# Output projection in the body as pairs of 64-row products, with a change of PSUM banks halfway

## The chip, the core and the metric

The kernel runs on one core of a Trainium2 chip. The metric is the device time of one execution in microseconds; the median of several runs is given, and one execution was profiled. The core's engines are TensorE (PE in the profile; its weight loads are PEld), VectorE (DVE), ScalarE (ACT), GpSimd (POOL) and SyncE (SP), which issues most of the DMAs.

## What is computed

For each of 8 batches, with S = 3200 rows, D = 256 columns and 64 inner columns:

```python
# stage 1, attention with squared ReLU, gated by u
scores = (1 / S) * z @ z.T                 # 3200 x 3200
x = u * (np.maximum(scores, 0.0) ** 2 @ v) # 3200 x 256
# stage 2, a mixing over the tokens, then the output projection
wq, wk = x @ w_q, x @ w_k                  # 3200 x 64 each
mixed = (1 / np.sqrt(64)) * (wq @ wk.T) @ x
out = np.maximum(mixed, 0.0) @ w_out       # 3200 x 256
```

Inputs and output are fp32; the kernel multiplies in fp16 and adds in fp32 in PSUM.

## The kernel before

**Tiling.** The 3200 rows of a batch are 25 tiles of 128, and seven groups: six of 512 rows (W) and one of 128 (LASTG). A step of the main product takes 64 of a tile's 128 rows on the upper half of TensorE's rows and the other 64 on the lower half: two products with 64 rows each, written `top(0)` and `top(1)`, that run side by side and add into two PSUM banks, acc{half}0 and acc{half}1. Nearly every product of the body has this 64-row form.

**The parts, by line.** `scores` (L224) makes a pair of score tiles, sc, in a PSUM tile of two banks. `first_stage` (L243 on ScalarE, L247 on VectorE) takes ReLU into g; `second_stage` (L260 on ScalarE, L262 on GpSimd) squares into at. Part of the tiles are turned by DMA transposes into tt (L282), as the score matrix is symmetric. `second_product` (L303) is the main product into acc. `gate` adds the two acc banks (L319 on ScalarE, then L320 on VectorE) and multiplies by u on GpSimd (L335). Then follow the transposed x (L349), the projections qk (L366, L379), the keys (L384), the heads hd (L393), and, a batch later, `mix` (L429), whose ReLU `mix_out` writes into rt on ScalarE (L446), and `proj` (L456), the output projection: for a group of 512 rows, four tiles of 128 rows times two chunks of 128 columns, 8 products of 128 rows each, against the weights wo. `proj_out` scales the two banks in one ScalarE pass (L484) into fo, and SP stores it (L485).

**PSUM.** The four acc banks are the main product's. The other four are two tiles of two banks each, tag ps, which sc, qk, hd, mx and fo take in turn.

**What sets the order.** The schedule is manual: every engine takes its instructions in the order in which the program writes them. A planner in Python writes them. It keeps a clock for TensorE, VectorE, ScalarE and GpSimd (`clock`), adds planned durations with `give`, and holds planned times for SP and the transfers (`sp_at`, `dma_at`, `moves`). Its main loop (L862 to L895) looks at TensorE's planned time and chooses what it does next: an "extra" (keys, heads, mix, proj), a score pair, or one step of the main product. Score pairs and extras need a free PSUM tile; `slots` holds the times at which the two tiles are planned to be free again, `open_slot` takes the first and `close_slot` puts a time back. Score pairs may run ahead of the main product by a lead of 140 steps. For a projection, `use_proj` plans 1.08 us of TensorE and 1.0 us of ScalarE for a large group. The plan only orders instructions; at run time semaphores hold each one until its data are there.

The body has 47 such projections, 40 of 512 rows and 7 of 128. Batch 7's own, and two groups of batch 6 that are kept back, are projected in the tail, behind the main loop, by `projected` and `proj`; the tail is the same before and after.

Of the kernel before, what the change touches and what calls it, by code (L numbers as in the profile page):

```python
# [10 lines left out]
FP32 = mybir.dt.float32  # L11
RELU = mybir.ActivationFunctionType.Relu
AOP = mybir.AluOpType
# [3 lines left out]
def kernel(  # L17
# [10 lines left out]
    nc = tc.nc  # L28

    B, S, D = u.shape  # L30
    dqk = z.shape[2]
    dh = moe_w_q.shape[1]
    P = 128
# [48 lines left out]
    def top(r):  # L82
        return slice(r * dqk, (r + 1) * dqk)
# [5 lines left out]
    def rows(t, b):  # L89
        return t[b].rearrange("(p n) d -> p n d", n=NT)  # L90
# [10 lines left out]
    def load_first_z():  # L101
        for i, (n0, nn) in enumerate(ZCH):
            z32[n0] = px.tile([P, nn, dqk], FP32, tag="x_sb", name="z32")
            queue = nc.scalar if i == 1 else nc.sync
            queue.dma_start(out=z32[n0][:], in_=rows(z, 0)[:, n0 : n0 + nn, :])
# [342 lines left out]
    def proj(b, gi, banks):  # L448
        rt = rts.pop((b, gi))
        nj = widths[gi] // P  # L450
        for r in halves(gi):
            n = min(2, nj - 2 * r)
            flat = rt[:, r, :, :].rearrange("p d s -> p (d s)")
            for dc in range(ND):
                for j in range(n):
                    nc.tensor.matmul(  # L456
                        out=banks[r][:, ds(j * D, D)],
                        lhsT=flat[:, ds((dc * n + j) * P, P)],
                        rhs=wo[:, dc, :],
                        start=(dc == 0 and j == 0),  # L460
                        stop=(dc == ND - 1 and j == n - 1),
                    )

    def proj_out(b, gi, banks, ways, stores=None):
        n0 = starts[gi] // P
        if stores is None:
            fo = pg.tile([P, 2, W], FP32, tag="g", name="fo")
        else:
            fo = pg.tile([P, 2, W], FP32, tag="fo", name="fo", bufs=2)
        flat_out = fo[:].rearrange("p a w -> p (a w)")  # L470
        at = 0
        for on_dve, queue, n in ways:
            sl = slice(at * D, (at + n) * D)
            if isinstance(banks, list):
                part = banks[at // 2][:, 0 : n * D]
            else:
                part = banks[:].rearrange("p a w -> p (a w)")[:, sl]
            if on_dve:
                nc.vector.tensor_scalar(
                    out=flat_out[:, sl], in0=part, scalar1=FINAL_SCALE, scalar2=None,  # L480
                    op0=AOP.mult,
                )
            else:
                nc.scalar.mul(out=flat_out[:, sl], in_=part, mul=FINAL_SCALE)  # L484
            store = lambda queue=queue, at=at, n=n, sl=sl: queue.dma_start(  # L485
                out=rows(out, b)[:, n0 + at : n0 + at + n, :],
                in_=flat_out[:, sl].rearrange("p (n d) -> p n d", d=D),
            )
            if stores is None:
                store()  # L490
            else:
                stores.append(store)
            at += n
# [29 lines left out]
    def give(engine, ready, weight):  # L523
        clock[engine] = max(clock[engine], ready) + weight
        return clock[engine] + HOP

    slots = [0.0, 0.0]
    free_at, row_at, blocks = {}, {}, {}
    pending, later, extras, keyed, kept = [], [], [], [], []
    out_of, turned_at, z_at = {}, {}, {}  # L530
    produced, stored = [0], []
    last = B - 1

    moves = []
    sp_at, dma_at = [0.0], [0.0]
    LANDS = 4.0
    RING = 2.0
# [34 lines left out]
            send(min(ripe, key=lambda x: x[1]))  # L572

    def open_slot():
        clock[PE] = max(clock[PE], slots.pop(0))

    def close_slot(t):
        slots.append(t)

    def cold():  # L580
        return 2.0 if clock[PE] < 11.0 else 1.0

    def use_pair():
        open_slot()
        p = produced[0]
        produced[0] += 1
        sc = scores(p)
        clock[PE] += 0.22 * cold()
        ready = clock[PE] + FROM_PE
        on_act = max(clock[ACT], ready) + BIAS < max(clock[DVE], ready)  # L590
        done = give(ACT, ready, 1.03) if on_act else give(DVE, ready, 1.2)
        g = first_stage(p, sc, on_act)
        close_slot(done)
        pending.append((done, p, g))

    def squares():
# [20 lines left out]
                row_at[b, gj, starts[gi] // P + n] = t + 0.5  # L617

    def use_keys(b, gi):
        open_slot()  # L620
        ps = ps_tile("qk")
        projections(b, gi, ps)
        clock[PE] += 0.44 if gi < LASTG else 0.24
        ready = clock[PE] + FROM_PE
        projections_out(b, gi, ps)
        done = give(ACT, ready, 0.56)
        n = widths[gi] / P
        move(
            done + SLACK, done + 10.0, 1.28, 0.21 * n, lambda: turn_keys(b, gi),
            lambda t: at_time(t, lambda: keys_landed(b, gi)), lambda: len(ks) < NK,  # L630
        )
        close_slot(done)

    FIRST_HEADS = range(3)

# [4 lines left out]
                add_extra(clock[PE] + 0.5, "heads", lambda gis=gis: use_heads(b, gis))  # L640

    def use_heads(b, gis):
        open_slot()
        ps = ps_tile("hd")
        heads(b, gis, ps)
        clock[PE] += 0.2 + 0.0547 * sum(widths[gi] // P for gi in gis)
        heads_out(b, ps)
        done = give(DVE, clock[PE] + FROM_PE, 0.7)
        close_slot(done)
        if gis is FIRST_HEADS:  # L650
            return
        done = give(DVE, done, 0.35)
        move(done + SLACK, done + 2.0, 0.55, 0.1, lambda: cross_heads(b, 0))
        move(
            done + SLACK, done + 2.0, 0.55, 0.1, lambda: cross_heads(b, 1),
            lambda t: at_time(t, lambda: crossed(b)),
        )
# [14 lines left out]
                    add_extra(t + 4.0 + 18.0 * i, "mix", lambda gi=gi: use_mix(b, gi))  # L672

    def use_mix(b, gi):
        open_slot()
        ps = ps_tile("mx")
        mix(b, gi, [ps[:, 0, :], ps[:, 1, :]])
        clock[PE] += 0.22
        mix_out(b, gi, ps)
        done = give(ACT, clock[PE] + FROM_PE, 1.03 if gi < LASTG else 0.3)  # L680
        close_slot(done)
        add_extra(done + 0.5, "proj", lambda: use_proj(b, gi))

    def use_proj(b, gi):
        open_slot()
        ps = ps_tile("fo")
        proj(b, gi, [ps[:, 0, :], ps[:, 1, :]])
        clock[PE] += 1.08 if gi < LASTG else 0.42
        stores = []
        proj_out(b, gi, ps, [(False, nc.sync, widths[gi] // P)], stores)  # L690
        done = give(ACT, clock[PE] + FROM_PE, 1.0 if gi < LASTG else 0.3)
        close_slot(done)
        stored.append(1e9)

        def landed(t, i=len(stored) - 1):
            stored[i] = t

        move(done + SLACK, done + 6.0, 0.55, 1.6, stores[0], landed)
# [128 lines left out]
        return all(x in used for x in tiles[2 * p : 2 * p + 2])  # L827

    make_identity(nc, ident)
    load_first_z()  # L830
    load_first_v(0, 2)
    cast_first(0)
# [29 lines left out]
    while groups or work or current["left"]:  # L862
        flush()
        squares()
        now = clock[PE]
        room = slots[0] <= now
        extra = next(
            (
                x
                for x in extras  # L870
                if x[0] <= now
                and (x[1] != "proj" or len(stored) < 2 or stored[-2] <= now)
                and (x[1] != "mix" or sum(y[1] == "proj" for y in extras) < 2)
            ),
            None,
        )
        p = produced[0]
        able = p < NPAIR and z_at[p_chunk(p)] <= now and (p < NAT or all_used(p - NAT) and turned_at.get(p - NAT, 0.0) <= now and not out_of.get(p - NAT))
        wanted = able and p * total < (done_acc + lead) * NPAIR
        room = room and calm(1.1)  # L880
        if room and extra and (not wanted or turn_about or extra[1] == "proj"):
            turn_about = False
            extras.remove(extra)
            extra[2]()
        elif room and wanted:
            turn_about = True
            use_pair()
        elif acc_step():
            done_acc += 1
        elif room and able:  # L890
            use_pair()
        else:
            marks = [slots[0], sp_at[0] - 0.4] + [x[0] for x in pending + later + extras + moves]
            marks += list(free_at.values()) + [t for t in row_at.values() if t > now][:50]
            clock[PE] = min([t for t in marks if t > now] + [now + 0.5])  # L895

    while extras or later or moves:
        x = next((x for x in extras if x[1] == "proj"), None)  # L900
        if not x:
            ripe = [x for x in moves if not x[6] or x[6]()]
            x = min(later + extras + ripe, key=lambda x: x[0])
        clock[PE] = max(clock[PE], x[0])
        if x in later:
            later.remove(x)
            x[1]()
        elif x in moves:
            send(x)
        else:  # L910
            extras.remove(x)
            x[2]()
# [74 lines left out]
```

## Time and profile before

| | us |
|---|---|
| median of 3 runs | 791.21 (791.0 to 795.83) |
| profiled execution, its time | 790.96 |
| its span, first to last instruction | 789.2 |
| TensorE busy (PE) | 763.2 (97%) |
| weight loads (PEld) | 645.7 (82%) |
| VectorE | 479.4 (61%) |
| ScalarE | 551.8 (70%) |
| GpSimd | 612.9 (78%) |

The granted TensorE clock is 0.994 in the mean. A busy TensorE is not TensorE at its peak, as products overlap and their ends are modelled. In a row of the groups or of the timeline stand the engine, the line, the operation, what it writes and reads, shapes, counts and times; "[0.21 <-issue]" is idle time ahead of an instruction and what ended it, "issue" being a wait for nothing that the profile shows. In the table of waits a row gives the sum in us, the times, and the longest.

### The profile page before, as it was taken

The numbers are of one execution on the slowest core, as the hardware profiler recorded it, in microseconds if no ns is written. First come the engines' busy times: TensorE is split into PE (matmuls) and PEld (weight loads), VectorE is DVE, ScalarE is ACT, GpSimd is POOL, SyncE is SP. The second block draws the span as 40 slices with busy tenths as digits, with TensorE's granted clock in tenths as the row PEclk, the third lists the DMA queues.
The fourth block names the chain that finished last, engine by engine and source line by source line (L and its number), as shares of the span: only waits on it lengthen the run. The fifth ranks groups of instructions, "written<-read, shape, count | busy, mean of one in ns | idle before, by whom it ended". The sixth has DMA issues, their size and how long they took to land.

```text
span 789.2 us, 28159 instructions
## 1 busy us (share of the span) xinstructions
PE 763.2 (97%) x12373; PEld 645.7 (82%) x12373; DVE 479.4 (61%) x479; ACT 551.8 (70%) x659; POOL 612.9 (78%) x418
## 2 busy tenths in 40 slices
PE   6989999999999999999999999999999999999976
PEld 5879898887888888888788887988788888888864
DVE  5755577664685656754587635666468654675634
ACT  5766478766776677786687678866778767777624
POOL 7887799886998769877798876888789775787830
PEclk9999999999999999999999999999999999999998
DMA  7999999999999979999999999999999998899425
GB/s 192 146 172 165 177 160 179 156 225 194 204 184 189 220 164 194 152 189 216 210 162 170 187 214 199 177 151 208 193 207 165 178 225 160 183 163 194 122 56 220
DMA packets 310636, 142.57 MB, mean 181 GB/s; under 512 B 287985, under 2 KB 291953, under 8 KB 310513
## 3 DMA queue, kind: packets, MB, share of 16 engines
q1 hardware_dynamic: 303600, 124.60, 83.4%
q0 software_dynamic: 6768, 15.98, 14.8%
q8 instruction: 96, 1.57, 0.9%
q14 instruction: 28, 0.22, 0.1%
q10 hardware_dynamic: 144, 0.20, 0.1%
HBM read 59.64 MB, written 26.21 MB: 109 GB/s over the span
## 4 chain that ended last, share of the span: by engine, by line
PE 91%; DVE 3%; DMA 2%; issue 1%; ACT 1%; POOL 1%; SPq 0%; DVEq 0%; POOLq 0%; ACTq 0%
PE acc L303 66%; PE sc L224 12%; PE fo L456 6%; PE qk L366 3%; DVE g L247 2%; PE hd L393 1%; PE mx L429 1%; DVE both L320 1%; DMA v_sb<-in_v_dram 1%; DMA hx<-ha 1%; ACT both L319 1%; POOL x_sb L335 1%; DVE ha L410 0%; DMA z<-in_z_dram 0%; SPq L349 0%
## 5 line engine op out<-in xcount | busy, mean ns | idle before, releaser
L262 POOL TENSOR_TENSOR at<-g 128x1024 f16<-128x1024 f32 (+2 forms) x245 | 451.5, 1858 | 82.5 <-DVE g L247 66.5
L303 PE MATMUL acc<-v_sb,at 64*128 64x256 f16 x7312 | 499.1, 270 | 5.0 <-DVE both L320 2.5
L247 DVE TENSOR_SCALAR g<-sc 128x1024 f32<-128x1024 f32 (+2 forms) x309 | 363.9, 1197 | 153.0 <-PE sc L224 137.6
L303 PEld LDWEIGHTS <-at 64*128 64x128 f16 x7312 | 393.0, 94 | 66.8 <-issue 12.7
L260 ACT ACTIVATE at<-g 128x1024 f16<-128x1024 f32 x223 | 229.4, 1036 | 30.7 <-DVE g L247 27.2
L243 ACT ACTIVATE g<-sc 128x1024 f32<-128x1024 f32 (+1 forms) x159 | 159.2, 1003 | 60.5 <-PE sc L224 59.8
L335 POOL TENSOR_TENSOR x_sb<-both,u_sb 128x512 f16<-128x512 f32 (+1 forms) x112 | 134.4, 1207 | 64.4 <-DVE both L320 63.8
L224 PE MATMUL sc<-zT 64*128 64x512 f16 x920 | 180.2, 378 | 3.5 <-DVE g L247 3.1
L303 PE MATMUL acc<-v_sb,tt 64*128 64x256 f16 x2304 | 158.7, 269 | 0.0
L320 DVE TENSOR_TENSOR both<-acc,both 128x512 f32<-128x512 f32 (+1 forms) x104 | 69.1, 670 | 128.9 <-ACT both L319 128.4
L303 PEld LDWEIGHTS <-tt 64*128 64x128 f16 x2304 | 123.3, 94 | 11.6 <-issue 0.4
L319 ACT COPY both<-acc 128x512 f32<-128x512 f32 (+1 forms) x104 | 58.4, 566 | 65.5 <-PE acc L303 63.5
L224 PEld LDWEIGHTS <-zT 64*128 64x128 f16 x920 | 56.8, 94 | 17.6 <-issue 12.4
L484 ACT ACTIVATE fo<-fo 128x1024 f32<-128x1024 f32 (+2 forms) x50 | 44.9, 908 | 23.5 <-PE fo L456 22.1
L446 ACT ACTIVATE rt<-mx 128x1024 f16<-128x1024 f32 (+1 forms) x49 | 45.1, 931 | 22.1 <-PE mx L429 21.8
L456 PE MATMUL fo<-wo,rt 128*128 128x256 f16 x400 | 53.1, 276 | 1.2 <-ACT rt L444 0.6
L456 PEld LDWEIGHTS <-rt 128*128 128x128 f16 x400 | 35.4, 98 | 15.6 <-issue 9.6
L379 ACT CAST qk<-qk 128x512 f16<-128x512 f32 (+1 forms) x54 | 29.4, 544 | 21.6 <-PE qk L366 21.6
L366 PE MATMUL qk<-xT_sb,wqk 64*128 64x256 f16 (+1 forms) x404 | 32.2, 265 | 0.1
L366 PEld LDWEIGHTS <-wqk 64*128 64x128 f16 x416 | 22.8, 94 | 2.5 <-issue 0.5
L303 PE MATMUL acc<-v_sb,ttl 64*128 64x256 f16 x384 | 24.6, 269 | 0.0
L303 PEld LDWEIGHTS <-ttl 64*128 64x128 f16 x384 | 19.7, 94 | 3.5 <-issue 0.8
(42 smaller groups left out, 163.9 us busy)
## 6 DMA issues: line engine op xcount, KB each, us to landing
u_sb<-in_u_dram SPq DMA_DIRECT2D x48, 512.0 KB, 5.1
out_dram<-fo SPq DMA_DIRECT2D x45, 512.0 KB, 4.7
v_sb<-in_v_dram POOLq DMA_DIRECT2D x35, 320.0 KB, 6.0
zn<-in_z_dram POOLq DMA_DIRECT2D x7, 400.0 KB, 5.7
tt<-at SPq DMA_TRANSPOSE x144, 4.4
out_dram<-fo SPq DMA_DIRECT2D x6, 256.0 KB, 2.1
u_sb<-in_u_dram SPq DMA_DIRECT2D x8, 128.0 KB, 3.9
hx<-ha SPq DMA_DIRECT2D x16, 64.0 KB, 4.7
```

What stands on the lines that cost most here:

```text
L224: nc.tensor.matmul(out=sc[:, h, 0:gw], lhsT=zT[b][top(h), ts(ti, P)], rhs=zT[b][top(h), ds(gs, gw)], start=True, stop=True,)
L243: nc.scalar.activation(out=g[:, hs, 0:w], in_=sc[:, hs, 0:w], func=RELU, scale=GSCALE)
L247: nc.vector.tensor_scalar(out=g[:, hs, 0:w], in0=sc[:, hs, 0:w], scalar1=0.0, scalar2=GSCALE, op0=AOP.max, op1=AOP.mult,)
L260: nc.scalar.square(out=out, in_=g[:, hs, 0:w])
L262: nc.gpsimd.tensor_mul(out=out, in0=g[:, hs, 0:w], in1=g[:, hs, 0:w])
L303: nc.tensor.matmul(out=accs[half, r][:, ds((j % 2) * D, D)], lhsT=weights(b, gi, ti, j)[top(r), :], rhs=vs[b][top(r), ti, :], start=(first ...
L319: nc.scalar.copy(out=both[:, 0 : n * D], in_=accs[half, 0][:, 0 : n * D])
L320: nc.vector.tensor_add(out=both[:, 0 : n * D], in0=accs[half, 1][:, 0 : n * D], in1=both[:, 0 : n * D])
L335: nc.gpsimd.tensor_mul(out=xs[b, gi][:, 0:n, :, r, :].rearrange("p n c d -> p (n c) d"), in0=both[:, 0 : n * D].rearrange("p (m d) -> p m ...
L366: nc.tensor.matmul(out=ps[:, r, 0 : n * P], lhsT=wqk[top(r), c, :, :].rearrange("p t h -> p (t h)"), rhs=xTs[b, gi][top(r), 0:n, c, :], st ...
L446: nc.scalar.activation(out=out, in_=ps[:, 0:nr, 0 : ND * n * P], func=RELU)
L456: nc.tensor.matmul(out=banks[r][:, ds(j * D, D)], lhsT=flat[:, ds((dc * n + j) * P, P)], rhs=wo[:, dc, :], start=(dc == 0 and j == 0), sto ...
```

## The change

The body's projections take the 64-row form. `proj_stage` runs in two stages for a large group. In stage 0 the upper 64 rows of the first half of the row tiles add into bank 0, and, side by side with them, the lower 64 rows of the second half into bank 1. In stage 1 the banks change places: the upper rows work for the second half, into bank 1, the lower rows for the first half, into bank 0. [...] The planner puts other work between the stages; stage 1 is a new kind of entry, `changes`, which the main loop takes first once its planned time has come. The PSUM tile stays taken until stage 1 has been scaled; an open tile has the time 1e9 in `slots`.

A group of 128 rows has one stage: each 64-row half has a bank of its own, and `small_proj_out` adds the two, ScalarE scaling one and VectorE adding the other. Two tiny tiles, signs, are cleared by GpSimd at the start. The planned times are 0.44 us of TensorE a stage and 0.22 us for a small group.

```diff
+    signs = [consts.tile([1, 2], FP32, tag=f"sign{i}", name=f"sign{i}") for i in range(2)]
+    SEES = mybir.DependencyInfo(mybir.DependencyClass.Sync, mybir.DependencyReason.DATA)
+
+    def proj_stage(b, gi, ps, stage, seen=None):
+        rt = rts[b, gi]
+        nj = widths[gi] // P
+        n = min(2, nj)
+        product = None
+        for dc in range(ND):
+            for j in range(n):
+                for r in range(2):
+                    bank = r ^ stage
+                    half = bank if nj > n else 0
+                    flat = rt[:, half, :, :].rearrange("p d s -> p (d s)")
+                    product = nc.tensor.matmul(
+                        out=ps[:, bank, ds(j * D, D)],
+                        lhsT=flat[top(r), ds((dc * n + j) * P, P)],
+                        rhs=wo[top(r), dc, :],
+                        start=(stage == 0 and dc == 0 and j == 0),
+                        stop=(dc == ND - 1 and j == n - 1 and (stage == 1 or nj == n)),
+                    )
+                    if seen is not None:
+                        tc.add_manual_dep(
+                            product.ins, seen.ins.name, SEES, reason="the change of halves"
+                        )
+                        seen = None
+        return product
+
+    def sign_off(product, on_act):
+        sign = signs[0 if on_act else 1]
+        copy = nc.scalar.copy if on_act else nc.vector.tensor_copy
+        seen = copy(out=sign[:, 1:2], in_=sign[:, 0:1])
+        tc.add_manual_dep(seen.ins, product.ins.name, SEES, reason="last before the change")
+        return seen
+
+    def small_proj_out(b, gi, ps, stores):
+        n0 = starts[gi] // P
+        fo = pg.tile([P, 2, W], FP32, tag="fo", name="fo", bufs=2)
+        nc.scalar.mul(out=fo[:, 0, 0:D], in_=ps[:, 0, 0:D], mul=FINAL_SCALE)
+        nc.vector.scalar_tensor_tensor(
+            out=fo[:, 0, 0:D], in0=ps[:, 1, 0:D], scalar=FINAL_SCALE, in1=fo[:, 0, 0:D],
+            op0=AOP.mult, op1=AOP.add,
+        )
...
-    slots = [0.0, 0.0]
+    slots = [[0.0], [0.0]]
...
+    moves, changes = [], []
+    SEEN = 0.1
...
     def open_slot():
-        clock[PE] = max(clock[PE], slots.pop(0))
-
-    def close_slot(t):
-        slots.append(t)
+        slot = slots.pop(0)
+        assert slot[0] < 1e9
+        clock[PE] = max(clock[PE], slot[0])
+        slot[0] = 1e9
+        slots.append(slot)
+        return slot
+
+    def close_slot(slot, t):
+        slot[0] = t
...
     def use_proj(b, gi):
-        open_slot()
+        slot = open_slot()
         ps = ps_tile("fo")
-        proj(b, gi, [ps[:, 0, :], ps[:, 1, :]])
-        clock[PE] += 1.08 if gi < LASTG else 0.42
+        whole = widths[gi] == W
+        product = proj_stage(b, gi, ps, 0)
+        clock[PE] += 0.44 if whole else 0.22
+        ready = clock[PE] + FROM_PE
+        if whole:
+            on_act = max(clock[ACT], ready) < max(clock[DVE], ready)
+            seen = sign_off(product, on_act)
+            t = give(ACT if on_act else DVE, ready, 0.08) + SEEN
+            changes.append((t, lambda: end_proj(b, gi, ps, slot, seen)))
+        else:
+            stores = []
+            small_proj_out(b, gi, ps, stores)
+            done = give(DVE, give(ACT, ready, 0.35), 0.4)
+            proj_ended(b, gi, slot, done, stores)
+
+    def end_proj(b, gi, ps, slot, seen):
+        proj_stage(b, gi, ps, 1, seen)
+        clock[PE] += 0.44
         stores = []
         proj_out(b, gi, ps, [(False, nc.sync, widths[gi] // P)], stores)
-        done = give(ACT, clock[PE] + FROM_PE, 1.0 if gi < LASTG else 0.3)
-        close_slot(done)
+        done = give(ACT, clock[PE] + FROM_PE, 1.0)
+        proj_ended(b, gi, slot, done, stores)
...
     make_identity(nc, ident)
+    for sign in signs:
+        nc.gpsimd.memset(sign[:], 0.0)
     load_first_z()
...
         now = clock[PE]
-        room = slots[0] <= now
+        if changes and changes[0][0] <= now:
+            changes.pop(0)[1]()
+            continue
+        room = slots[0][0] <= now
...
```

More of the change, by code (lines that the diff above doesn't have):

```diff
@@ L462, in proj @@
                     )
+    signs = [consts.tile([1, 2], FP32, tag=f"sign{i}", name=f"sign{i}") for i in range(2)]
[38 more added lines that the diff above has]
+        )
+        stores.append(
+            lambda: nc.sync.dma_start(out=rows(out, b)[:, n0, :], in_=fo[:, 0, 0:D])
+        )
     def proj_out(b, gi, banks, ways, stores=None):
@@ L532 @@
     last = B - 1
-    moves = []
+    moves, changes = [], []
+    SEEN = 0.1
     sp_at, dma_at = [0.0], [0.0]
@@ L592, in use_pair @@
         g = first_stage(p, sc, on_act)
-        close_slot(done)
+        close_slot(slot, done)
         pending.append((done, p, g))
@@ L619, in use_keys @@
     def use_keys(b, gi):
-        open_slot()
+        slot = open_slot()
         ps = ps_tile("qk")
@@ L631, in use_keys @@
         )
-        close_slot(done)
+        close_slot(slot, done)
     FIRST_HEADS = range(3)
@@ L642, in use_heads @@
     def use_heads(b, gis):
-        open_slot()
+        slot = open_slot()
         ps = ps_tile("hd")
@@ L648, in use_heads @@
         done = give(DVE, clock[PE] + FROM_PE, 0.7)
-        close_slot(done)
+        close_slot(slot, done)
         if gis is FIRST_HEADS:
@@ L674, in use_mix @@
     def use_mix(b, gi):
-        open_slot()
+        slot = open_slot()
         ps = ps_tile("mx")
@@ L680, in use_mix, with proj_ended @@
         done = give(ACT, clock[PE] + FROM_PE, 1.03 if gi < LASTG else 0.3)
-        close_slot(done)
+        close_slot(slot, done)
         add_extra(done + 0.5, "proj", lambda: use_proj(b, gi))
     def use_proj(b, gi):
-        open_slot()
+        slot = open_slot()
         ps = ps_tile("fo")
-        proj(b, gi, [ps[:, 0, :], ps[:, 1, :]])
-        clock[PE] += 1.08 if gi < LASTG else 0.42
+        whole = widths[gi] == W
[15 more added lines that the diff above has]
+        clock[PE] += 0.44
         stores = []
         proj_out(b, gi, ps, [(False, nc.sync, widths[gi] // P)], stores)
-        done = give(ACT, clock[PE] + FROM_PE, 1.0 if gi < LASTG else 0.3)
-        close_slot(done)
+        done = give(ACT, clock[PE] + FROM_PE, 1.0)
+        proj_ended(b, gi, slot, done, stores)
+    def proj_ended(b, gi, slot, done, stores):
+        rts.pop((b, gi))
+        close_slot(slot, done)
         stored.append(1e9)
@@ L892 @@
         else:
-            marks = [slots[0], sp_at[0] - 0.4] + [x[0] for x in pending + later + extras + moves]
+            marks = [slots[0][0], sp_at[0] - 0.4]
+            marks += [x[0] for x in pending + later + extras + moves + changes]
             marks += list(free_at.values()) + [t for t in row_at.values() if t > now][:50]
             clock[PE] = min([t for t in marks if t > now] + [now + 0.5])
-    while extras or later or moves:
+    while extras or later or moves or changes:
         x = next((x for x in extras if x[1] == "proj"), None)
-        if not x:
+        if changes:
+            x = changes[0]
+        elif not x:
             ripe = [x for x in moves if not x[6] or x[6]()]
@@ L904 @@
         clock[PE] = max(clock[PE], x[0])
-        if x in later:
+        if x in changes:
+            changes.remove(x)
+            x[1]()
+        elif x in later:
             later.remove(x)
```

## The prediction

> **What bounds the kernel now.** I read the page first: the shares of the engines, the chain that ended last, the DMA queues.
>
> ```profile
> span 789.2 us, 28159 instructions
> PE 763.2 (97%) x12373; PEld 645.7 (82%) x12373; DVE 479.4 (61%) x479; ACT 551.8 (70%) x659; POOL 612.9 (78%) x418
> ...
> PEclk9999999999999999999999999999999999999998
> ...
> q1 hardware_dynamic: 303600, 124.60, 83.4%
> q0 software_dynamic: 6768, 15.98, 14.8%
> ...
> PE 91%; DVE 3%; DMA 2%; issue 1%; ACT 1%; POOL 1%; SPq 0%; DVEq 0%; POOLq 0%; ACTq 0%
> PE acc L303 66%; PE sc L224 12%; PE fo L456 6%; PE qk L366 3%; DVE g L247 2%; PE hd L393 1%; PE mx L429 1%; DVE both L320 1%; DMA v_sb<-in_v_dram 1%; DMA hx<-ha 1%; ACT both L319 1%; POOL x_sb L335 1%; DVE ha L410 0%; DMA z<-in_z_dram 0%; SPq L349 0%
> ```
>
> TensorE holds 91% of the chain at a clock of 0.9 or more almost to the end, so time taken out of its instruction stream in the body comes out of the kernel, as long as nothing else is nearly as full. The DMA queues add up to 98% of their engines' span; that is the one competitor, and it comes back among the rivals.
>
> Next, the table of waits, for what TensorE itself waits for, and how ready the engines behind it are.
>
> ```profile
> DVE g L247 <- PE sc L224: 137.6, 139, 4.4
> ...
> ACT g L243 <- PE sc L224: 59.8, 58, 3.1
> ...
> ACT fo L484 <- PE fo L456: 22.1, 33, 2.6
> ...
> PE sc L224 <- DVE g L247: 3.1, 5, 0.8
> ...
> PE acc L303 <- DVE both L320: 2.5, 6, 0.5
> ...
> PE acc L303 <- DMA v_sb<-in_v_dram: 1.5, 1, 1.5
> ```
>
> Others wait for TensorE, it hardly waits for them: a score pair stood 5 times for the VectorE read that frees its PSUM tile, 3.1 us in all. VectorE and ScalarE mostly stand ready when a product ends.
>
> Then the timeline around one projection, the place of the change.
>
> ```profile
> 201.42 1.58 PE L303 MATMUL acc<-v_sb,at 64*128 64x256 f16 x26
> ...
> 202.93 0.77 PEld L456 LDWEIGHTS <-rt 128*128 128x128 f16 x8 [0.21 <-issue]
> 202.94 1.05 PE L456 MATMUL fo<-wo,rt 128*128 128x256 f16 x8
> ...
> 203.91 0.10 PEld L224 LDWEIGHTS <-zT 64*128 64x128 f16 x2 [0.21 <-issue]
> 203.91 0.39 PE L224 MATMUL sc<-zT 64*128 64x512 f16 x2
> ...
> 204.02 1.02 ACT L484 ACTIVATE fo<-fo 128x1024 f32<-128x1024 f32 x1 [1.22 <-PE fo L456]
> ...
> 204.42 1.22 DVE L247 TENSOR_SCALAR g<-sc 128x1024 f32<-128x1024 f32 x1 [1.78 <-PE sc L224]
> ...
> 205.34 0.38 PE L224 MATMUL sc<-zT 64*128 64x512 f16 x2
> ...
> 209.91 2.13 PE L303 MATMUL acc<-v_sb,at 64*128 64x256 f16 x36
> ```
>
> The last row gives the pace of 64-row products: 36 of them are 18 pairs, a pair's two members side by side on the upper and lower rows; one product lasts 0.27 us (270 ns in the groups below), so 17 steps take 2.13 - 0.27 = 1.86 us, 0.1094 us a pair. The 8 full products have the same pace: (1.05 - 0.27) / 7 = 0.111 us. So a full product does in one step just what a pair of half products does in one step: the change gains nothing on the arithmetic. But the weight load stands still for 0.21 us ahead of the projection and again behind it, waiting for nothing the profile shows. In matmul starts: the last pair ahead starts at 201.42 + 1.58 - 0.27 = 202.73, the next product behind at 203.91, 1.18 us later; nine steps of 0.1094 are 0.98. **One visit to 128-row products costs 0.20 us of standing still.**
>
> How many visits? The line's own view for 150 to 757 us (the body; the tail keeps the old form):
>
> ```profile
> L456 PE MATMUL fo<-wo,rt x334: 272/273/283, 157.6 to 745.7; 128*128 128x256 f16 x167
> ...
>   issue: 8.4, 40
>   PE sc L224: 0.2, 1
> ```
>
> and from the groups of the page, the length of one product and the counts of score products and of gates:
>
> ```profile
> L303 PE MATMUL acc<-v_sb,at 64*128 64x256 f16 x7312 | 499.1, 270 | 5.0 <-DVE both L320 2.5
> ...
> L224 PE MATMUL sc<-zT 64*128 64x512 f16 x920 | 180.2, 378 | 3.5 <-DVE g L247 3.1
> ...
> L320 DVE TENSOR_TENSOR both<-acc,both 128x512 f32<-128x512 f32 (+1 forms) x104 | 69.1, 670 | 128.9 <-ACT both L319 128.4
> ```
>
> The double visit:
>
> ```profile
> 250.92 0.29 PE L303 MATMUL acc<-v_sb,at 64*128 64x256 f16 x2
> ...
> 251.14 1.92 PE L456 MATMUL fo<-wo,rt 128*128 128x256 f16 x16
> ...
> 252.99 0.28 PE L303 MATMUL acc<-v_sb,at 64*128 64x256 f16 x2
> ```
>
> 334 products are 40 projections of 512 rows (8 each) and 7 of 128 rows (2 each). Some stand back to back, as the x16 row does: 252.99 - 250.93 = 2.06 us against 17 steps = 1.85, again one 0.20, not two. Hence 41 waits on entry, 41 visits: 41 x 0.20 = **8.2 us**.
>
> **The change part by part.**
>
> *The projections as 64-row pairs.* 8 products become 16 in 8 pairs, 2 become 4 in 2 pairs; 8 and 2 steps of 0.109 as before, and no visit: -8.2 us. The bounds: -8.2 if all go, 0 if the standing still has another cause.
>
> *The change of halves.* 40 times the second half of the pairs waits for a one-element copy, itself waiting for the last product of the first half. Its price on its engine is not in this trace; the nearest rows:
>
> ```profile
> L243 ACT ACTIVATE g<-sc 128x128 f32<-128x128 f32 x3 | 0.8, 275 | 3.9 <-PE sc L224 3.9
> ...
> L247 DVE TENSOR_SCALAR g<-sc 128x128 f32<-128x128 f32 x5 | 1.4, 285 | 2.1 <-PE sc L224 2.0
> ...
> L320 DVE TENSOR_TENSOR both<-acc,both 128x256 f32<-128x256 f32 x8 | 3.4, 423 | 7.3 <-ACT both L319 7.3
> ...
> L484 ACT ACTIVATE fo<-fo 128x256 f32<-128x256 f32 x7 | 2.7, 386 | 0.3 <-PE fo L456 0.3
> ```
>
> 128 elements a partition take 0.28 us on either engine; with 1024 taking 1.22 (the DVE row at 204.42), an element costs (1.22 - 0.285) / 896 = 1.04 ns and the fixed part is 0.15 us. So the copy costs 0.15 to 0.28; I take 0.16, being nearest to no elements. 40 of them are 6.4 us on two engines that are 61% and 70% busy: hidden. The round trip: after the first half's last pair, TensorE's next step is due 0.109 us after that pair starts, and the product ends 0.16 later; ScalarE starts 0.03 us after a product ends (203.99 to 204.02), VectorE 0.12 (204.30 to 204.42); the copy 0.16; back to a weight load 0.03 to 0.1 (an estimate from the same two rows). Sum 0.4 to 0.55 us. The written order releases the second half 0.57 us after the first (0.27 + 0.08 + 0.12 + 0.1, the plan's own constants FROM_PE, the copy's weight, HOP and SEEN), and fills those five steps with second products. So on plan TensorE stands 0. What is queued behind a late copy is everything: TensorE takes matmuls in order. For how often a plan like this is late, the nearest rows are the two waits above: 3.1 us for 460 score pairs (x920), 2.5 us for 104 gates (x104), scaled to 40 events 0.3 and 1.0 us. **+0.3 us**, since the copy may choose the freer engine and the gate may not; ends 0 and, if each waits a whole score read, 40 x 1.2 = 48.
>
> *The PSUM tile is held longer.* Now from 202.94 to 205.04, 2.1 us. Then: 0.44 + 0.57 + 0.44 + 0.16 + 0.03 + 1.02 = 2.66. 40 x 0.56 = 22 us of one of two tiles, for which score pairs wait. The cover is the second products, which need no such tile; the score after next starts at 205.34, 0.3 us after release, so it is delayed, and made up later, since score pairs otherwise find their tile free (5 waits). I take 0; ends 0 and +22.
>
> *Small projections.* One VectorE pass (423 ns row) is added behind the ScalarE pass (386 ns row), 7 times, and the PSUM tile is kept 0.5 us longer; no product waits there. 0, at most 7 x 0.5 = 3.5.
>
> *The two memsets.* On POOL, ahead of the first loads of v.
>
> ```profile
> 0.74 0.20 POOL masks.py:197 MEMSET ident<- 128x128 f16 x1 [0.29 <-POOLq L971]
> ...
> 1.45 0.72 POOL L108 DMA_DIRECT2D v_sb<-in_v_dram  x1
> ...
> 3.74 0.50 POOL L120 CAST zd<-z 128x384 f16<-128x384 f32 x1 [1.57 <-DMA z<-in_z_dram]
> ```
>
> Two at no more than 0.20 us, and POOL then idles 1.57 us for z: 0; without that cover +0.4. Stores, loads and transposes keep their number; the stores are issued about 0.5 us later, into waits SP has anyway.
>
> The sum: the profiled execution took 790.96 us (span 789.2 and 1.8 around it), 0.25 under the median 791.21. 791.2 - 8.2 + 0.3 = **783.3**; I say 783.2.
>
> [...]
>
> **The rivals.**
>
> *The copy is late (slower).* Place: the first weight load of the second half. The planned clocks hold true only if ScalarE or VectorE reaches the copy at once. Each full pass that stands unplanned ahead of it costs TensorE up to 1.0 to 1.2 us. Break-even is 8.2 / 40 = 0.2 us a change of halves; from 0.4 on the kernel is 8 us slower. If half of the copies sit behind a 1.2 us pass: 24 us, 783 + 24 - 0.3 = 807; if a third, 799. For it: 70% and 61% busy engines and a bare 0.02 to 0.15 us of margin. Against it: ScalarE idled for the product ahead of its scaling pass 33 times, VectorE for the scores 139 times.
>
> *PSUM becomes the bound (slower).* If the 22 us of holding reached TensorE in full: 791 - 8 + 22 = 805; it decides from 37% of that. Against it stand the 5 waits and second products as filler. [...]
>
> *Transfers are the bound anyway.* At 98% of the queues' share a body 1% shorter may just wait for blocks: 791. Against it: 1.5 us of TensorE waiting for a transfer of v, at the start, and SP waits for sources, not for room:
>
> ```profile
> SPq L282 <- ACT at L260: 50.4, 30, 5.9
> ```
>
> *It doesn't do what it says.* If halves took turns instead of running side by side, each half product costs its own step: 334 x 0.109 = +36, 819. The x36 row speaks against it.
>
> **How the numbers follow.** Forecast and its neighbours (779 to 787.5): 0.68. Transfers, or a gain mostly lost to small waits (787.5 to 800): 0.12. Late copy 0.12, PSUM 0.06, taking turns 0.02. One per cent is 7.9 us, about what a measurement of this kernel can tell from no change; that line, 783.3, runs through the middle of the forecast's own range, slightly on the good side as the sum with 0 for late copies is 783.0: 0.45 faster, 0.23 same of the 0.68. With 0.10 of the lost gains inside 1%: same 0.33; slower 0.12 + 0.06 + 0.02, and 0.02 of the lost gains, 0.22. The range 779 to 803 leaves out 0.04 below (an order of work that happens to fall better) and 0.13 above: about half of the late copy, half of PSUM, and taking turns, with little else.
>
> **What would show it.** Right: no 0.21 us "issue" gap at body projections, only at the tail's; product rows 64x256 at the old pace; TensorE busy the same but the span 8 us shorter; waits for the copy under 1 us in all. Wrong: a row "PE fo" or "PEld" waiting for the copy with several us; score pairs waiting for PSUM reads more than 5 times; rows waiting for tt or x transfers.

## The result

The changed kernel takes 799.5 us in the median of 8 runs, the kernel before 793.1 on the same chip; the ratio is 1.0081, its 95% interval 1.0063 to 1.0098. It is slower by 0.8%, where 1% faster was forecast. The page of the kernel after (same lines as those shown of before):

```profile
span 797.9 us, 28897 instructions
PE 761.7 (95%) x12707; PEld 672.6 (84%) x12707; DVE 470.4 (59%) x500; ACT 562.8 (71%) x686; POOL 613.2 (77%) x419
...
PEclk9999999999999999998999999999999999999998
...
PE 86%; DVE 4%; DMA 3%; ACT 3%; issue 1%; POOL 1%; SPq 1%; DVEq 0%; POOLq 0%; ACTq 0%
```

TensorE falls from 91% to 86% of the chain, DMA and ScalarE rise from 2% and 1% to 3% each, and in one slice the clock reads 8 tenths where before it reads 9. The busy time by stretches (columns: stretch and its length; busy time and instructions of PE, PEld, DVE, ACT, POOL; granted clock; DMA share; GB/s) has the place; the row of before stands first, then that of after:

```profile
300.00:400.00 100.00, 99.35 (x1650) 83.99 (x1646) 60.31 (x61) 71.59 (x85) 80.50 (x55) 1.00 1.07 188
```

```profile
300.00:400.00 100.00, 90.17 (x1490) 79.81 (x1486) 52.72 (x59) 64.06 (x79) 68.53 (x45) 0.95 0.95 163
```

Between 300 and 400 us all engines, and the transfers, do less, most of them by about a tenth. The table of waits of after (sign, L498, is the one-element copy of `sign_off`, written behind stage 0 on ScalarE or VectorE; stage 1's first product waits for it):

```profile
DVE sign L498 <- PE fo L481: 21.4, 22, 2.5
...
ACT fo L534 <- DMA out_dram<-fo: 8.2, 1, 8.2
...
PE sc L224 <- ACT fo L534: 7.2, 1, 7.2
...
PE acc L303 <- DVE both L320: 4.6, 11, 0.5
...
PE qk L366 <- issue: 2.0, 1, 2.0
```

Two single events stand out: a scaling pass of ScalarE that waited 8.2 us for a store, and a score product that waited 7.2 us for that pass. (The 2.0 us at a qk product come up in the last section.) The timeline of after shows how they hang together:

```profile
358.90 1.02 ACT L534 ACTIVATE fo<-fo 128x1024 f32<-128x1024 f32 x1 [1.16 <-PE fo L481]
...
362.86 0.38 ACT L505 ACTIVATE fo<-fo 128x256 f32<-128x256 f32 x1 [0.72 <-PE fo L481]
...
363.06 0.62 PE L481 MATMUL fo<-wo,rt 64*128 64x256 f16 x8
...
364.65 0.53 SPq L535 DMA_DIRECT2D out_dram<-fo  x1
...
364.92 0.40 PE L224 MATMUL sc<-zT 64*128 64x512 f16 x2
365.28 0.38 SPq L511 DMA_DIRECT2D out_dram<-fo  x1
...
371.46 1.02 ACT L534 ACTIVATE fo<-fo 128x1024 f32<-128x1024 f32 x1 [8.22 <-DMA out_dram<-fo]
372.51 0.33 SPq L535 DMA_DIRECT2D out_dram<-fo  x1
372.53 0.61 PE L224 MATMUL sc<-zT 64*128 64x512 f16 x2 [7.21 <-ACT fo L534]
```

A large projection is scaled by 359.9, a small one from 362.9 on (L505), and another large one ends its products at 363.7. Each needs one of the two fo tiles. The first one's store is issued by SP only at 364.65, and lands 6.7 us later (the longest landing of the six stores around it), near 371.4; only then may the third pass (L534) write, and it holds the PSUM tile that the next score pair needs. TensorE stands from 365.3 to 372.5; the next main products start at 372.91, behind that pair. The kernel before did not start a projection until the store before last had landed on plan (the main loop's test on `stored`). The change enters a projection in `stored` only when its second half is written, so a projection that is still open is not counted, and the test looks one store too far back.

### The profile page after: what moved, and what is told of

The parts are those of the page before. It is cut to its first block, busy times and chain, and to the rows that moved or that the text cites. A ratio compares the mean times of both kernels' runs of the same rounds, so it can differ in the third digit from the quotient of the medians.

```text
span 797.9 us, 28897 instructions
## 1 busy us (share of the span) xinstructions
PE 761.7 (95%) x12707; PEld 672.6 (84%) x12707; DVE 470.4 (59%) x500; ACT 562.8 (71%) x686; POOL 613.2 (77%) x419
## 4 chain that ended last, share of the span: by engine, by line
PE 86%; DVE 4%; DMA 3%; ACT 3%; issue 1%; POOL 1%; SPq 1%; DVEq 0%; POOLq 0%; ACTq 0%
PE acc L303 63%; PE sc L224 12%; PE fo L481 4%; PE qk L366 3%; DVE g L247 2%; DVE both L320 1%; PE hd L393 1%; PE mx L429 1%; PE fo L456 1%; ACT both L319 1%; DMA hx<-ha 1%; DMA out_dram<-fo 1%; DMA z<-in_z_dram 1%; DMA kx<-qk 1%; ACT g L243 1%
## 5 line engine op out<-in xcount | busy, mean ns | idle before, releaser
L303 PE MATMUL acc<-v_sb,at 64*128 64x256 f16 x7312 | 514.9, 270 | 7.4 <-DVE both L320 4.6
L262 POOL TENSOR_TENSOR at<-g 128x1024 f16<-128x1024 f32 x244 | 451.6, 1867 | 82.9 <-DVE g L247 66.0
L303 PEld LDWEIGHTS <-at 64*128 64x128 f16 x7312 | 409.8, 94 | 59.6 <-issue 17.7
L260 ACT ACTIVATE at<-g 128x1024 f16<-128x1024 f32 (+1 forms) x224 | 229.1, 1030 | 25.5 <-DVE g L247 22.2
L243 ACT ACTIVATE g<-sc 128x1024 f32<-128x1024 f32 (+2 forms) x169 | 169.4, 1004 | 70.7 <-PE sc L224 69.7
L224 PE MATMUL sc<-zT 64*128 64x512 f16 (+1 forms) x920 | 185.8, 380 | 9.3 <-ACT fo L534 7.2
L303 PE MATMUL acc<-v_sb,tt 64*128 64x256 f16 x2304 | 172.0, 269 | 0.0
L320 DVE TENSOR_TENSOR both<-acc,both 128x512 f32<-128x512 f32 (+1 forms) x104 | 69.2, 670 | 125.1 <-ACT both L319 118.6
L319 ACT COPY both<-acc 128x512 f32<-128x512 f32 (+1 forms) x104 | 58.3, 565 | 42.8 <-PE acc L303 39.8
L534 ACT ACTIVATE fo<-fo 128x1024 f32<-128x1024 f32 (+1 forms) x43 | 42.3, 994 | 39.9 <-PE fo L481 25.9
L481 PE MATMUL fo<-wo,rt 64*128 64x256 f16 x668 | 52.5, 269 | 0.0
L481 PEld LDWEIGHTS <-rt 64*128 64x128 f16 x668 | 36.7, 94 | 2.5 <-issue 0.2
```

What stands on the lines that cost most here:

```text
L224: nc.tensor.matmul(out=sc[:, h, 0:gw], lhsT=zT[b][top(h), ts(ti, P)], rhs=zT[b][top(h), ds(gs, gw)], start=True, stop=True,)
L243: nc.scalar.activation(out=g[:, hs, 0:w], in_=sc[:, hs, 0:w], func=RELU, scale=GSCALE)
L260: nc.scalar.square(out=out, in_=g[:, hs, 0:w])
L262: nc.gpsimd.tensor_mul(out=out, in0=g[:, hs, 0:w], in1=g[:, hs, 0:w])
L303: nc.tensor.matmul(out=accs[half, r][:, ds((j % 2) * D, D)], lhsT=weights(b, gi, ti, j)[top(r), :], rhs=vs[b][top(r), ti, :], start=(first ...
L319: nc.scalar.copy(out=both[:, 0 : n * D], in_=accs[half, 0][:, 0 : n * D])
```

## The experiments

Theory 1: this one stall, with the clock's lapse behind it (a mean of 0.53 from 369 to 376 us), makes the kernel slower; the standing still at the visits is really gone. Rival, theory 2: the halves' waits cost a little everywhere, and the stall only takes up slack. All ratios are to the kernel before on the same chip.

**e_small_tile.** The small projection gets another tile, so that the third pass finds a free fo tile. All instructions keep their order.

```diff
-        fo = pg.tile([P, 2, W], FP32, tag="fo", name="fo", bufs=2)
+        fo = psml.tile([P, 1, D], FP32, tag="hx", name="fos", bufs=1)   # small_proj_out
```

> The changed kernel with the small projections' result in a tile of its own, so that the two fo tiles serve the large ones alone; every engine's instructions stand in the same order. Theory 1 (the store of an earlier result holds the third fo tile, once, for 7.2 us of TensorE, and the clock lapse behind it costs 1.7): the one 8.2 us wait of the scaling pass for a store is gone, time 799.5 - 9 = 790 to 791, clear of the changed kernel, level with before. Theory 2 (the halves' waits cost a little everywhere, the one stall only takes up slack): 797 to 800.

Measured: 788.8 us, ratio 0.9959 (0.9938 to 0.9980). No scaling pass waits for a store. That is 1.2% of 792.6, near 10 us, below the changed kernel, from one buffer: theory 1 holds and theory 2 falls. (The 2.0 us wait at a qk product and the clock behind it, 3.6 us together in the profile of after, are absent here too; without them after would still take some 796 us.) And it is 0.4% faster than before, not the 1% forecast.

**e_guard.** The planner's test mended in place of the buffer.

```diff
     def use_proj(b, gi):
         slot = open_slot()
+        stored.append(1e9)
+        turn = len(stored) - 1
...
-        stored.append(1e9)          # in proj_ended
```

> The changed kernel with the planner's list of stores entered when a projection begins, as in the kernel before, not when its second half ends, so that the planner again waits for the store before last ahead of a new projection. The order of work changes. Theory 1: no wait of a scaling pass for a store, 787 to 792. Theory 2: 797 to 800.

Measured: 790.7 us, 0.9967 (0.9946 to 0.9989); no scaling pass waits for a store. The cause is thus shown from both sides, buffer and plan.

**e_full_rows.** Is a visit's price real? In `proj_stage`, for large groups:

```diff
-        for dc in range(ND):
+        for dc in range(ND if nj > n else 0):
+            flat = rt[:, stage, :, :].rearrange("p d s -> p (d s)")
+            for j in range(n):
+                product = nc.tensor.matmul(
+                    out=ps[:, stage, ds(j * D, D)],
+                    lhsT=flat[:, ds((dc * n + j) * P, P)],
+                    rhs=wo[:, dc, :],
...
```

> As e_small_tile, but the large projections' two stages are 4 full 128-row products each, one bank a stage, with the copy and the order left as they are. It makes 80 visits to 128-row products. If a visit costs 0.20 us of the end (the prediction's term): e_small_tile + 16 us, about 806. If the gap at a visit is hidden or costs nothing at the end: within 3 us of e_small_tile.

Measured: 805.4 us, 1.0155 (1.0126 to 1.0183); 16.5 us over e_small_tile, 16.5 / 80 = **0.21 us a visit**, where the prediction read 0.20 off one place of the trace. By its timeline the visits are 76, as four times two stages stand back to back: 0.22. The two times are known to a few tenths of a per cent, so the second digit is not firm.

**e_at_once.** The price of the round trip, laid bare.

```diff
-            changes.append((t, lambda: end_proj(b, gi, ps, slot, seen)))
+            clock[PE] = t
+            end_proj(b, gi, ps, slot, seen)
```

> As e_small_tile, but the second stage is written straight behind the copy, with no other products between: it lays the round trip through the copy bare, 40 times. By the prediction's 0.4 to 0.55 us from step to step, less one step of 0.11: e_small_tile + 12 to 18 us, with 40 visible waits of TensorE on the copy of 0.3 to 0.45 us. If the round trip is far longer (the rival of a late copy): + 30 us or more.

Measured: 803.3 us, 1.0133 (1.0101 to 1.0166), 14.4 over e_small_tile. Its waits:

```profile
PE fo L481 <- ACT sign L498: 7.9, 21, 0.5
PE fo L481 <- DVE sign L498: 6.1, 19, 1.5
```

14.0 us in 40 waits, 0.35 each: as estimated. In the profile of the changed kernel no product waits for a copy at all, so the work written between the halves does cover it.

**What took the rest of the gain?** Of the 8 us, e_small_tile shows 3 to 4. TensorE's waits between 150 and 757 us, first of before, then of e_small_tile:

```profile
PE sc L224 <- DVE g L247: 2.0, 3, 0.8
PE mx L429 <- DVE g L247: 0.5, 1, 0.5
PE acc L303 <- DVE both L320: 0.2, 1, 0.2
```

```profile
PE acc L303 <- DVE both L320: 2.3, 6, 0.5
PE sc L224 <- DVE g L247: 1.6, 2, 1.3
PE acc L303 <- ACT both L319: 0.9, 1, 0.9
PE qk L366 <- DVE g L247: 0.4, 1, 0.4
PE qk L366 <- ACT qk L379: 0.4, 1, 0.4
```

2.7 us have become 5.6, and the new ones wait mostly for the gate (L319, L320), which empties the acc banks: 0.2 before, 3.2 now. Four explanations were tried: the longer hold of the PSUM tile (H), mere order (O), second halves in the gate's way (C), engines blocked at the copy (B).

**e_hold and e_nudge**, on the kernel before:

```diff
-        close_slot(done)
+        close_slot(done + (0.56 if gi < LASTG else 0.0))               # e_hold
...
-        clock[PE] += 1.08 if gi < LASTG else 0.42
+        clock[PE] += 1.06 if gi < LASTG else 0.40                      # e_nudge
```

> The kernel before, with one planned time changed: the PSUM tile of a large projection counts as free 0.56 us later than it is. Products, copies and buffers stay as before; only the order in which work is written moves. Theory H (the longer hold takes away the score pairs and extras that fill TensorE while the two acc banks are being emptied at the end of a half; this ate some 4 of the 8.2 us): before + 3 to 5 us, with TensorE's waits on the gate's two passes (L319, L320) between 150 and 757 us up from 0.2 to 2 or more. Theory O (only the luck of another order, with no link to the hold): within 2 us of before, or either way, like e_nudge.

> The kernel before, with a projection planned at 1.06 us of TensorE in place of 1.08 (0.40 in place of 0.42): another order of the same work for no reason, as a measure of what order alone moves. Both theories: within 3 us of before; what it moves is what e_hold has to exceed.

Measured: e_hold 793.5 us, 1.0006 (0.9987 to 1.0024); e_nudge 796.8, 1.0038 (1.0016 to 1.0059). Freeing the tile later on plan does nothing to the full-row form (the gate waits are 0.8 us, not 2 or more), so H is not borne out there; a change of 0.02 us in one planned duration, for no reason, moves the kernel by 3 us. That is the size of what is to be explained.

**e_split and e_seen**, on e_small_tile: one bank of the scaling pass moved to VectorE, and `SEEN = 0.0` for 0.1.

```diff
-        proj_out(b, gi, ps, [(False, nc.sync, widths[gi] // P)], stores)
+        nc.scalar.mul(out=fo[:, 0, :], in_=ps[:, 0, :], mul=FINAL_SCALE)       # e_split
+        nc.vector.tensor_scalar(out=fo[:, 1, :], in0=ps[:, 1, :], scalar1=FINAL_SCALE, scalar2=None, op0=AOP.mult)
...
-    SEEN = 0.1
+    SEEN = 0.0                                                                  # e_seen
```

> As e_small_tile, but the scaling of a large projection is one bank on ScalarE (about 0.58 us) beside the other on VectorE (0.69) in place of both banks on ScalarE (1.02), so that the PSUM tile is free 0.35 us earlier. Theory H: the gate waits fall, 2 to 3 us under e_small_tile, 786 to 787. Theory O: within 1.5 us of e_small_tile, either way.

> As e_small_tile, with the second half planned 0.1 us earlier (SEEN 0). By e_at_once the first product of a second half starts at the earliest some 0.5 us after the last pair of the first one, so at 0.47 + 0.11 us on plan TensorE should still not wait for the copy: no row of waits on the copy over 0.5 us in all, time within 2 us of e_small_tile. If the copies are late on the chip: 40 x 0.1 = 4 us or more above it.

Measured: e_split 793.1 us, 0.9998 (0.9986 to 1.0011): by the ratios 0.39%, 3 us, more than e_small_tile. That is outside what either theory allowed. The tile is in fact held for less time (1.79 us in the mean from the start of the copy to the end of the scaling, 2.21 in e_small_tile), so the result speaks against H as put; but it also adds 40 passes to VectorE, and score products now wait for them:

```profile
PE sc L224 <- DVE fo L765: 1.8, 6, 0.3
```

e_seen: 786.0 us, **0.9934 (0.9903 to 0.9964)**, the fastest form measured, under both kernels, though its interval overlaps that of e_small_tile. Its profile still has no product waiting for a copy: the planned 0.57 us had room.

**e_guard_seen, e_seen_late, e_nudge_up**: three more orders (e_guard with SEEN 0; e_small_tile with SEEN 0.2; before with 1.10 and 0.44).

> e_guard (the list of stores entered when a projection begins, both fo tiles shared as in the changed kernel) with the second half planned 0.1 us earlier. Theory 1 with order luck of 3 us either way: 786 to 792, no wait of a scaling pass for a store over 1 us. If the stall comes back in this order: 797 or more.

> e_small_tile with the second half planned 0.1 us later (SEEN 0.2): another order of the 64-row form. If the rest of the gain is lost to the order: anywhere in 785 to 794, without relation to SEEN. If holding the PSUM tile is what costs: 4 us or more above e_small_tile, some 793, as e_seen lay 3 below it.

> The kernel before with a projection planned at 1.10 us in place of 1.08: a third order of the full-row form. By the spread of before, e_hold and e_nudge: 790 to 798, and above the mean of the 64-row orders without the stall (788.8, 790.7, 786.0).

Measured: 789.7 us, 0.9975 (0.9955 to 0.9994); 793.5, 1.0003 (0.9985 to 1.0020); 792.6, 1.0002 (0.9985 to 1.0019). The first and third came as expected. The second lies inside both of its ranges and so decides nothing; besides, e_seen_late has the unmended test, and the store wait is back in its order, in a milder form, of which 1.2 us reach TensorE:

```profile
ACT fo L534 <- DMA out_dram<-fo: 4.7, 2, 3.1
...
PE sc L224 <- ACT fo L534: 1.2, 1, 1.2
```

**e_calm and e_sign_late**, on e_small_tile: second halves kept from the end of a half of the main product, and the copy written later.

```diff
-        if changes and changes[0][0] <= now:
+        if changes and changes[0][0] <= now and (calm(1.0) or changes[0][0] + 2.0 <= now):  # e_calm
...
-            seen = sign_off(product, on_act)
+            changes.append((ready, lambda: mid_proj(b, gi, ps, slot, product)))  # e_sign_late: sign_off there
```

> As e_small_tile, but the plan holds a second half back (for 2 us at most) while the end of a half of the main product is near, as it already does with score pairs and whole projections. Theory C (second halves and their 1.0 us scaling pass get in the way of the gate, which frees the acc banks): TensorE's waits on the gate between 150 and 757 us fall from 3.2 us to under 1, time 785 to 787. If the gate waits come from elsewhere: within 3 us of e_small_tile, waits as before.

> As e_small_tile, but the copy is written into ScalarE's or VectorE's order 0.27 us later on plan, when the first half is about to end, so that no engine stands at the copy with other work behind it. Theory B (engines blocked at the copy delay the gate and the score reads): VectorE's wait at the copy falls from 21 us to under 8 and TensorE's waits with it, 785 to 787. If the blocked time costs nothing: within 3 us of e_small_tile, as another order would.

Measured: e_calm 795.6 us, 1.0047 (1.0028 to 1.0067); e_sign_late 792.4, 1.0010 (0.9980 to 1.0040). Neither gains anything, and both lie above every range that was expected (e_small_tile + 3 us at most). C falls: in e_calm the gate waits stay at 3.6 us and the waits for score reads rise to 5.9. The tile is held longer (2.39 us in the mean, counted as above), which would do this but is not shown to:

```profile
PE sc L224 <- DVE g L247: 5.9, 9, 1.3
PE acc L303 <- DVE both L320: 2.3, 6, 0.5
...
PE acc L303 <- ACT both L319: 1.3, 2, 0.9
```

In e_sign_late VectorE's time at the copy hardly falls, so it tests B only weakly and leaves it unproved, and two scaling passes wait for stores again (3.7 us).

```profile
DVE sign L498 <- PE fo L481: 19.7, 18, 2.0
...
ACT fo L534 <- DMA out_dram<-fo: 3.7, 2, 1.9
```

**What the starts of TensorE's products say.** The table of waits counts idle time from the end of the product ahead, 0.27 us after its start, although the next step is due 0.109 us after that start. So each wait is 0.16 us longer than its row says, and short ones don't show. Take instead the starts, from the 1400th to the 9990th main product, a stretch that holds the same products in all orders (the projections of before being 334 whole products or 668 half ones). Call a product late if it starts more than 0.1 us after its step is due, a step being 0.109 us, and twice that behind a score product; the two gaps of a visit are shorter and don't count. In the profiled executions, in us:

| | late starts, sum | of these, main products | the stretch without late starts |
|---|---|---|---|
| four orders of the full-row form | 4.7 to 8.7 (before 5.3) | 1.5 to 3.3, in 5 to 9 starts | 640.6 to 641.4 |
| eight of the 64-row form, without the long stall | 8.3 to 19.2 (e_small_tile 11.7) | 4.7 to 7.9, in 12 to 21 starts | 632.5 to 633.0 |

The last column differs by about 8 us between the forms and by 1 to 2 within a form (e_nudge_up, with 641.4, has 1.7 us of lower clock in it, 4.0 x 0.43 by the last section): every order of the 64-row form has the whole gain of the visits. What the orders differ by is late starts, and the times of the eight stand in the order of their sums, from e_seen with 8.3 to e_calm with 19.2. Late main products grew in all eight; the rest, score pairs and qk for the most part, goes with the order. e_seen has as many late main products as e_small_tile (6.8 and 6.9 us) and no late score pair (2.7 in e_small_tile).

What stays open: why main products start late more often in the 64-row form. In ratios, four orders of the full-row form lie between 1.0000 and 1.0038, and eight of the 64-row form between 0.9934 and 1.0047. In the series e_seen, e_small_tile, e_seen_late, e_calm the second half comes ever later and the time rises with it (ratios 0.9934, 0.9959, 1.0003, 1.0047), which fits a cost of the held tile. But e_hold and e_split do not fit it, nor does e_guard, which gains nothing from the same step (0.9967, with SEEN 0 0.9975), and e_seen_late has the store wait in it. The runs don't settle it.

## Why the prediction was wrong, point by point

- *TensorE is the bound, and a visit costs 0.20 us.* Right: 0.21 from 80 added visits. (In before, the 334 products stand in 42 stretches, not 41; it makes no difference to the sum.) The gaps at the body's projections are gone; for the new form the whole trace shows

```profile
PEld L481 <- issue: 0.2, 1, 0.2
```

- *The copy.* Right in mechanism and near in size. 0.16 us was taken; VectorE needs 0.142 and ScalarE 0.186 in the median:

```profile
L498 DVE COPY sign<-sign x24: 131/142/143, 178.0 to 745.9; 1x1 f32<-1x1 f32 x24
L498 ACT COPY sign<-sign x16: 173/186/191, 158.3 to 751.5; 1x1 f32<-1x1 f32 x16
```

 TensorE's waits for it were put at 0.3 us and were nothing. (The margin of 0.02 to 0.15 us should read 0.02 to 0.17, from 0.57 less 0.4 to 0.55.) The rival of a late copy, with 0.12, was not what made the kernel slower. That the second half has to wait for the first at all is not shown: no run leaves the copy out.
- *"Stores, loads and transposes keep their number; the stores are issued about 0.5 us later, into waits SP has anyway."* **This step failed.** It counted the stores and not what counts on them: the later entry in `stored` switches off, for an open projection, the test that kept three results from two tiles. It cost 7.2 us of TensorE, and a clock of 0.53 in the mean from 369 to 376 us (last section). Buffer and plan each take the whole effect away.
- *-8.2 us at the end of the kernel.* The term was right: without late starts the stretch is 8 us shorter in each of the eight orders. **The sum lacked a term**, and so only 3 to 4 us are left once the stall is mended: from before to e_small_tile the late starts grow by 6.4 us (11.7 less 5.3). The prediction scaled two rows of small waits to 40 copies and so looked only at the copy; waits for the gate and for score reads were taken to stay as they were. Why they grew is open.
- *The PSUM tile held longer, 0.* Open, as above; the runs that bear on it do not agree.
- *Transfers are the bound anyway.* Not as put; but a transfer's latency, the 6.7 us of one store, came onto the path where a buffer ran out.
- *The account of the profiled runs:* 790.96 to 799.66 is +8.7: -8.2 for the visits, +7.2 for the stall, +2.0 for a single "issue" wait in a qk product, some +3 for the clock (both in the last section), and 4.7 left, about what the other late starts grew by in after (4.4 us).

## What to carry to other kernels

When a part is split in two in a planned order, look for every list and test that the old end of the part fed: a guard on buffers that is entered later is a guard that is off in between. Price a removed gap at the place of the gap, but expect a tuned order to hand back part of it, and before reading a result of a few us, move the order for no reason and see how far that alone goes (here up to 3 us). Add up late starts of the engine that is the bound, and not only its idle time. A wait that appears once in a table, with a length of many us, is worth more than all averages: start there.

## What the runs showed of the hardware that was not expected

In after two stalls were paid a second time, in the clock. The stretches behind the first and across the second (columns as above):

```profile
328.00:332.00 4.00, 4.00 (x44) 3.39 (x42) 1.22 (x2) 2.91 (x4) 0.00 (x0) 0.60 1.33 197
...
369.00:376.00 7.00, 3.47 (x32) 2.65 (x33) 0.00 (x0) 3.10 (x3) 0.00 (x0) 0.53 0.59 167
```

The second belongs to the 7.2 us stall: a mean of 0.53 over 7 us is half speed for 6.6 of them, from 369 to about 375.6 (in slices of 0.5 us the clock reads 1.00 up to 368.5, 0.50 from 369 to 375.5 and 1.00 from 376 on). So TensorE runs on at half speed for 3.1 us after it could start again at 372.5 (8 to 10 products in such a slice, 14 ahead of the stall), which costs some 1.6 us, an estimate from 3.1 x 0.50. The first follows a stall of only 2 us and costs 4.0 x 0.40 = 1.6. e_small_tile, the same order without either stall, has a clock of 1.00 between 300 and 400 us. The other executions agree: the mean clock is 0.985 to 0.990 in all eight of the changed kernel, and 0.992 to 0.996 in all of e_small_tile and e_guard. At the 7.2 us stall half speed begins 3.5 us in, near 368.8, and ends 3.1 us behind it; at the 2.0 us stall it begins only as the stall ends, near 327.8, and lasts to about 331.2. Why it begins where it does is not shown. The shorter stall is not the only one of its length. In e_nudge_up a wait of 2.0 us is followed by a lower clock too:

```profile
519.90 0.39 PE L224 MATMUL sc<-zT 64*128 64x512 f16 x2 [2.00 <-DVE g L247]
```

```profile
521.00:525.00 4.00, 4.00 (x46) 3.41 (x42) 2.34 (x2) 1.02 (x1) 3.93 (x3) 0.57 1.23 229
```

In the profiled executions of e_nudge and e_seen_late the longest waits for a score read are 1.9 and 1.8 us, and the mean clock is 0.995 and 0.994; in that of e_nudge_up it is 0.992.

The 2 us stall of after itself stands in the middle of the 8 products of one qk, ahead of a weight load, and waits for nothing that the profile shows:

```profile
325.15 0.49 PE L366 MATMUL qk<-xT_sb,wqk 64*128 64x256 f16 x5
...
327.68 0.48 PE L366 MATMUL qk<-xT_sb,wqk 64*128 64x256 f16 x3 [2.04 <-issue]
```

What made it is not settled; no run here was aimed at it.
